# One attention and FFN kernel, one core: TensorE's order taken from a searched list

## The chip, the cores and the metric

The kernel runs on one core of a Trainium2 chip. The metric is the device time of one execution in microseconds, and the kernel before takes 229.23 us (median of 3 runs, 228.51 to 230.21). The *span* is the time from the first to the last instruction in the trace.

## The reference, cut to what matters

```python
B, H, S, D = 4, 8, 768, 64            # n_sink = 4, window = 128
keep = is_sink | in_window            # the first 4 keys, or the last 128
a = softmax(where(keep, q @ k.T / sqrt(D), -1e9));   x = a @ v
x = x.transpose(0, 2, 1, 3).reshape(3072, 512)
h = x @ w_in                          # 512 x 2048
g = h * sigmoid(beta * h)
out = g @ w_out                       # 2048 x 512
```

The kernel works on eight half batches of 384 tokens. A *unit* is one pair of heads of one half batch, so there are 32. The FFN of a half batch needs the attention of that half batch alone. That gives TensorE something to do while other engines work on the next attention.

## The kernel before

The program isn't written in its final order. Operations are added to a graph with their planned durations, and a planner inside the kernel's Python code decides which engine takes an operation that has alternatives and in which order each engine runs. The chip then executes these fixed orders, with semaphores. Before the change, TensorE's next group was decided by rules: at each step the first ready head of several streams, with margins, then a second pass that may pull one of eight groups ahead.

```python
while True:                                   # first pass: which stream next
    ...
    for s in tuple(PRIO) + ffn:               # OT, AV, SS, SC, T, then FFN
        h = head(s)
        if h[0] + mg <= now:
            best = (now, s, h[1]); break
    ...
for i, grp in enumerate(todo_pe[:self.SKIP]): # second pass: SKIP = 8
    ...
    if best is None or t < best[0] - self.SLACK:
        best = (t, "pe", i)
```

Some operations have alternatives with planned times (ns). They include a mask multiplication and a weight piece's cast from float32 to bf16:

```python
any_of(copies(dst, src_, {"act": 947, "dve": 602, "gp": 1060}), ...)    # one weight piece
any_of({"gp": (fn, 1150), "dve": (fn, 335)}, ...)                       # E * maskS
alts["dve"] = (lambda e: e.tensor_tensor(d, d, mk, ALU.mult), 70 + 256 * len(at_) / 1.9)   # E * maskT
add("sp", lambda e: e.dma_start(dst, src), 610, ...)                    # 192 KB of q or k
```

Weights arrive in 16 pieces of 512 KB. Half batches 0, 1 and 2 have q and k transposed by TensorE (`XB` = 3), and later ones by transposing DMAs ("crossbar"). Where the plan saw a gap at the start, TensorE got filler matmuls on a tile of ones.

The softmax here doesn't subtract the row's maximum and nothing guards it: scores larger than these inputs give would overflow.

Of the kernel before, what the change touches and what calls it, by code (L numbers as in the profile page):

```python
# [22 lines left out]
PAR = {'AHEAD': 0,  # L23
 'BACKLOG': 3000,
 'KEEP': 1000,
 'KEPT': 1,
 'MARGIN': 0,
 'MD': 1,
 'M_AV': 0,
 'M_H': 0,  # L30
 'M_O': 0,
 'M_OT': 500,
 'M_SC': 1000,
 'M_SS': 500,
 'M_T': 0,
 'PB': 2,
 'RAW': 0,
 'SPLIT': 0,
 'XB': 3,
 'l0': [4, 0, 3, 2, 1, 7, 5, 8, 10, 6, 9],  # L40
 'mix': 'awwwwwwwaawaaaaawaaawwawwwwwaaaa',
 'prio': ('OT', 'AV', 'SS', 'SC', 'T')}


class Op:
    __slots__ = ("eng", "fn", "deps", "signal", "count", "waits", "sem", "vc", "dma", "seq", "end", "ns", "alts",
                 "group", "tail", "preds", "ready", "left", "succ", "at", "queue", "ring", "lag")


class Graph:  # L50





    ENGINES = ("pe", "act", "dve", "gp", "sp")
    HOP = 180
    SKIP = 8
    SLACK = 50
    LEAD = 6000  # L60
    PAD = 1500
    BIAS, EARLY = 0, 10000

    COLD, WARM = 217, 150
    RING, FETCH = 165, 1100

    def __init__(self):
        self.ops = []
        self.writers = {}
        self.readers = {}  # L70
        self.last_x = {}
        self.reset()
        self.group = 0
        self.filler, self.fill_to = None, 0

    def reset(self):
        self.free = {e: 800.0 for e in self.ENGINES}
        self.dma_free = 0.0
        self.pending = []
        self.n_pe = 0  # L80

    def begin(self):

        self.group += 1

    def add(self, eng, fn, ns=0, r=(), w=(), x=(), dma=None, alts=None, queue=470, ring=64, lag=0, after=()):
# [3 lines left out]
        if alts:  # L90
            fn, ns = alts[eng]
        o.eng, o.fn, o.dma, o.ns, o.alts = eng, fn, dma, ns, alts or {eng: (fn, ns)}
        o.queue, o.ring, o.lag = queue, ring, lag
        o.signal, o.count, o.waits, o.vc = False, 0, [], None
        o.group = self.group if eng == "pe" else None
        o.seq = len(self.ops)
# [8 lines left out]
        for k in x:  # L105
            deps += [(p, False) for p in self.last_x.get(k, ())]
# [7 lines left out]
        for k in x:  # L114
            self.last_x[k] = [o] if eng == "pe" else self.last_x[k] + [o]
        at = self.free[eng]
        for p, _ in deps:
            at = max(at, p.end + (0 if p.eng == eng and not p.dma else self.HOP))
        self.place(o, at)
        self.ops.append(o)  # L120
        return o

    def fill(self, fn, r):

        def one():
            o = Op()
            o.eng, o.fn, o.dma, o.ns = "pe", fn, None, self.filler[0]
            o.signal, o.count, o.waits, o.vc = False, 0, [], None
            o.deps = [(p, True) for k in r for p in self.writers[k]]
            return o  # L130
        self.filler, self.fill_to = (self.COLD, one), self.group

    def place(self, o, at):
        o.at = at
        if o.dma:
# [11 lines left out]
            o.end = self.dma_free + 950 + (self.PAD if at > 45000 else 0)  # L147
        else:
            if o.eng == "pe":
                self.n_pe += 2  # L150
                if self.n_pe % 256 == 0:
                    self.dma_free = max(self.dma_free, at) + self.FETCH
            o.end = self.free[o.eng] = at + o.ns

    def at(self, keys):

        t = 0.0
        for k in keys:
            ws = self.writers.get(k)
            if not ws:  # L160
                return None
            t = max([t] + [p.end + self.HOP for p in ws])
        return t

    def bank_at(self, k):
        return max([0.0] + [p.end + self.HOP for p in self.last_x.get(k, ())])

    def arrange(self):


        ops = self.ops
        prev = None
# [6 lines left out]
        after = None  # L179
        for o in reversed(ops):  # L180
            o.tail = max([s.tail + self.HOP for s in o.succ] + [0.0])
            if o.eng == "pe":
                o.tail = max(o.tail, after.tail if after else 0.0)
                after = o
            o.tail += o.ns + (2000 if o.dma else 0)
        groups = {}
        for o in ops:
            if o.eng == "pe":
                groups.setdefault(o.group, []).append(o)
        todo_pe = list(groups.values())  # L190
        self.reset()
        new, planned = [], set()

        def ready(o, e):
            return max([0.0] + [p.end + (0 if p.eng == e and not p.dma else self.HOP) for p in o.preds])

        def done(o):
            planned.add(id(o))
            new.append(o)
            for s in o.succ:  # L200
                s.left -= 1
                if s.left == 0 and s.eng != "pe":
                    pool.append(s)

        pool = [o for o in ops if o.left == 0 and o.eng != "pe"]
        while todo_pe or pool:
            best = None
            for i, grp in enumerate(todo_pe[:self.SKIP]):
                own = set(map(id, grp))
                if any(id(p) not in planned and id(p) not in own for o in grp for p in o.preds):  # L210
                    continue
                t, off = self.free["pe"], 0.0
                for o in grp:
                    t = max([t] + [p.end + self.HOP - off for p in o.preds if id(p) not in own and p.eng != "pe"])
                    off += o.ns
                if best is None or t < best[0] - self.SLACK:
                    best = (t, "pe", i)
                if t <= self.free["pe"]:
                    break
            by_eng = {}  # L220
            for o in pool:
                opts = []
                for e, (fn, ns) in o.alts.items():
                    t = max(self.free[e], ready(o, e))
                    if o.dma:
                        t = max(t, self.dma_free - self.LEAD)
                    opts.append((t + ns + (self.BIAS if e == "act" and t < self.EARLY else 0), t, e))
                _, t, e = min(opts)
                by_eng.setdefault(e, []).append((t, o))
# [7 lines left out]
            if e == "pe":  # L237
                grp = todo_pe.pop(what)
                while self.filler and grp[0].group <= self.fill_to and self.free["pe"] + self.filler[0] <= t:
                    o = self.filler[1]()  # L240
                    self.place(o, max([self.free["pe"]] + [p.end + self.HOP for p, _ in o.deps]))
                    new.append(o)
                    if self.free["pe"] > 5000:
                        self.filler = (self.WARM, self.filler[1])
                if grp[0].group > self.fill_to:
                    self.filler = None
                for o in grp:
                    self.place(o, max([self.free["pe"]] + [p.end + self.HOP for p in o.preds if p.eng != "pe"]))
# [8 lines left out]
        for i, o in enumerate(new):  # L257
            o.seq = i

# [85 lines left out]
def bass_streamingllm_window__then__act_swish_beta_kernel(  # L345
# [34 lines left out]
    G.arrange()  # L380
# [13 lines left out]
def _program(nc, G, sb, ps, q, k, v, w_in, w_out, beta, out):  # L394
# [3 lines left out]
    RAW, PB = PAR.get('RAW', 1), PAR.get('PB', 2)  # L398
# [10 lines left out]
    def kind(hb):  # L409
        return "block" if hb in PARTS else "pair" if hb < PB else "whole" if hb < XB else "xbar"  # L410
# [4 lines left out]
    identF = sb("identF", (128, 128), F32)  # L415
# [27 lines left out]
    tt = sb("t", (128, HALF), F32, NTT)  # L443
    osb = sb("osb", (128, NOUT), F32, NOS)
    seen = sb("seen", (128, 12, 4), F32)
    G.touch = []
    G.touch.append((seen[:, 0:4, :], w_in.rearrange("(c p) f -> p c f", p=128)[:, :, 0:4]))
    G.touch.append((seen[:, 4:12, :], w_out.rearrange("(m p) n -> p m n", p=128)[:, 0:16:2, 0:4]))
# [8 lines left out]
    def tokens(hb, hp, i, rows, t0, n):  # L457
        if kind(hb) in ("pair", "whole"):
# [7 lines left out]
    def mark_t(hb, hps, cs):  # L466
        for hp in hps:
            for i in range(2):
                for c in cs:
                    G.writers["T", hb, hp, i, c] = G.writers["qkT", hb % (NT // 4), hp, i, c]  # L470

    def needs(u):
        hb, hp, c0, c1 = UNITS[u]
        ks = [c0 - 1] + list(range(c0, c1)) if c0 or hb % 2 else list(range(c0, c1))
        return [(hb if c >= 0 else hb - 1, hp, i, c % NK) for i, cs in ((0, range(c0, c1)), (1, ks)) for c in cs]

    def any_of(alts, r=(), w=(), x=()):

        return G.add(min(alts, key=lambda e: G.free[e] + alts[e][1] + (
            G.BIAS if e == "act" and G.free[e] < G.EARLY else 0)), None, 0, r, w, x, None, alts)  # L480
# [13 lines left out]
    w_in_src = w_in.rearrange("(c p) f -> p c f", p=128)  # L494
    w_out_src = w_out.rearrange("(m p) n -> p m n", p=128)
# [8 lines left out]
    held, kept = {7}, set()  # L504

    def choose(n):

        if n == 2:
            return min(((max(G.bank_at(("B", i)), G.bank_at(("B", i + 1))), [i, i + 1]) for i in range(7)
                        if not held & {i, i + 1}), default=None)  # L510
        if n == 4:
# [735 lines left out]
```

## Time and profile before

| | busy us | share of 226.9 us |
|---|---|---|
| TensorE | 216.4 | 95% |
| ScalarE | 153.8 | 68% |
| VectorE | 138.4 | 61% |
| GpSimd | 66.4 | 29% |

TensorE's 95% includes fillers and waits hidden inside pipelined matmuls. A better measure for this kernel, used in the prediction and below, is the *loss*. Take any matmul's start in the trace. Subtract what all useful matmuls ahead of it in the program occupy, by the start-to-start distances that the prediction lists (0.216 us for 512 columns, 0.187 us for entering and leaving a score block, and so on). What remains is time in which TensorE did nothing useful. In the kernel before, this loss is 7.7 us by 10 us, 12.5 by 20, 17.2 by 42, and 17.9 at the end.

### The profile page before, as it was taken

The numbers are of one execution on the slowest core, as the hardware profiler recorded it, in microseconds if no ns is written. First come the engines' busy times: TensorE is split into PE (matmuls) and PEld (weight loads), VectorE is DVE, ScalarE is ACT, GpSimd is POOL, SyncE is SP. The second block draws the span as 40 slices with busy tenths as digits, with TensorE's granted clock in tenths as the row PEclk, the third lists the DMA queues.
The fourth block names the chain that finished last, engine by engine and source line by source line (L and its number), as shares of the span: only waits on it lengthen the run. The fifth ranks groups of instructions, "written<-read, shape, count | busy, mean of one in ns | idle before, by whom it ended". The sixth has DMA issues, their size and how long they took to land.

```text
span 226.9 us, 4543 instructions
## 1 busy us (share of the span) xinstructions
PE 216.4 (95%) x1746; PEld 123.1 (54%) x1769; DVE 138.4 (61%) x304; ACT 153.8 (68%) x277; POOL 66.4 (29%) x155
## 2 busy tenths in 40 slices
PE   7979878999999999999999999999999999999994
PEld 5655446456555565655555555545554565555543
DVE  2898969756894678826887666654452455733310
ACT  2878998449786777748887756676585776744441
POOL 8450455012222663432225541020243630000000
PEclk9999999999999999999999999999999999999999
DMA  7999999999969999999999999511113121011112
GB/s 163 265 364 361 339 248 337 350 282 238 226 121 240 215 227 233 230 219 220 196 252 196 229 208 207 136 49 46 35 49 81 49 81 35 4 46 46 46 49 92
DMA packets 95845, 39.78 MB, mean 175 GB/s; under 512 B 82368, under 2 KB 88784, under 8 KB 95824
## 3 DMA queue, kind: packets, MB, share of 16 engines
q1 hardware_dynamic: 94256, 39.47, 74.1%
q8 instruction: 14, 0.23, 0.4%
q10 hardware_dynamic: 1568, 0.02, 0.4%
q14 instruction: 7, 0.06, 0.1%
HBM read 27.30 MB, written 6.29 MB: 148 GB/s over the span
## 4 chain that ended last, share of the span: by engine, by line
PE 81%; DVE 9%; ACT 5%; DMA 2%; issue 1%; SPq 0%
PE P L942 36%; PE P L920 32%; PE P L791 4%; PE P L871 4%; DVE onorm L878 2%; DVE g L927 2%; ACT E L800 2%; ACT t L925 2%; DMA k_stage<-in_k_dram 2%; PE P L861 1%; PE P L828 1%; PE P L700 1%; DVE k L543 1%; DVE E L817 1%; ACT qkT L538 1%
## 5 line engine op out<-in xcount | busy, mean ns | idle before, releaser
L925 ACT ACTIVATE t<-P,hbeta 128x384 f32<-128x384 f32 x128 | 73.2, 585 | 38.7 <-PE P L920 33.4
L927 DVE SCALAR_TENSOR_TENSOR g<-t,P 128x384 bf16<-128x384 f32 x128 | 69.1, 550 | 45.7 <-ACT t L925 43.9
L920 PE MATMUL P<-xT,w_in 128*128 128x384 bf16 x512 | 96.1, 326 | 0.0
L942 PE MATMUL P<-w_out,g 128*128 128x512 bf16 (+2 forms) x377 | 90.4, 370 | 1.2
L806 POOL TENSOR_SCALAR_AFFINE_SELECT E<-E 128x256 bf16<-128x256 bf16 x109 | 54.5, 529 | 94.1 <-ACT E L800 93.7
L920 PEld LDWEIGHTS P<-xT,w_in 128*128 128x128 bf16 x512 | 48.5, 98 | 36.8 <-DVE w_in L543 0.6
L942 PEld LDWEIGHTS P<-w_out,g 128*128 128x128 bf16 x400 | 36.8, 98 | 35.0 <-issue 0.5
L800 ACT ACTIVATE E<-P 128x768 bf16<-128x768 f32 x64 | 45.7, 768 | 4.1 <-PE P L791 4.1
L538 ACT ACTIVATE osb<-P 128x512 f32<-128x512 f32 (+2 forms) x24 | 13.9, 581 | 14.1 <-PE P L942 13.9
L871 PE MATMUL P<-vaug,E 128*128 128x65 bf16 x352 | 18.6, 193 | 1.4 <-DVE vaug L543 1.4
L871 PEld LDWEIGHTS P<-vaug,E 128*128 128x128 bf16 x352 | 16.6, 97 | 4.3 <-DVE vaug L543 1.7
L878 DVE TENSOR_TENSOR onorm<-P,rden 128x384 bf16<-128x384 f32 x32 | 17.8, 556 | 0.9
L791 PE MATMUL P<-qkT 64*128 64x128 bf16 (+1 forms) x256 | 15.9, 239 | 0.4 <-ACT E L800 0.2
L832 ACT ACTIVATE ES<-P 128x128 bf16<-128x128 f32 (+1 forms) x32 | 12.0, 402 | 4.3 <-PE P L828 4.3
L791 PEld LDWEIGHTS P<-qkT 64*128 64x128 bf16 x256 | 8.5, 94 | 11.2 <-issue 5.6
L876 DVE RECIPROCAL rden<-P 128x6 f32<-128x6 f32 x32 | 6.1, 191 | 12.5 <-PE P L871 12.4
L543 DVE CAST vaug<-v_stage 128x512 bf16<-128x512 f32 x22 | 10.8, 491 | 3.6 <-DMA v_stage<-in_v_dram 3.4
L543 DVE CAST q<-q_stage 128x512 bf16<-128x512 f32 (+1 forms) x20 | 9.6, 484 | 5.2 <-DMA q_stage<-in_q_dram 5.2
L861 PE MATMUL P<-vS,ES 128*128 128x130 bf16 x64 | 12.7, 221 | 0.0
L817 DVE TENSOR_TENSOR E<-E,maskS 128x512 bf16<-128x512 bf16 x16 | 7.7, 482 | 5.9 <-ACT E L800 5.1
L543 DVE CAST k<-k_stage 128x512 bf16<-128x512 f32 (+1 forms) x20 | 9.3, 469 | 3.0 <-DMA k_stage<-in_k_dram 2.9
L1173 PE MATMUL P<-ones 128*128 128x256 bf16 x44 | 8.8, 341 | 1.1 <-POOL ones L549 1.1
(50 smaller groups left out, 93.2 us busy)
## 6 DMA issues: line engine op xcount, KB each, us to landing
v_stage<-in_v_dram SPq DMA_DIRECT2D x24, 256.0 KB, 4.8
out_dram<-osb SPq DMA_DIRECT2D x23, 256.0 KB, 2.6
q_stage<-in_q_dram SPq DMA_DIRECT2D x15, 256.0 KB, 4.7
k_stage<-in_k_dram SPq DMA_DIRECT2D x15, 256.0 KB, 5.1
wst<-in_moe_w_in_dram SPq DMA_DIRECT2D x5, 512.0 KB, 6.9
wst<-in_moe_w_out_dram SPq DMA_DIRECT2D x4, 512.0 KB, 8.7
g<-in_moe_w_out_dram SPq DMA_DIRECT2D x4, 512.0 KB, 7.0
q_stage<-in_q_dram SPq DMA_DIRECT2D x8, 192.0 KB, 6.0
```

What stands on the lines that cost most here:

```text
L538: return lambda e: e.activation(dst, src, AF.Copy, bias=0.0, scale=scale)
L543: return lambda e: e.tensor_copy(dst, src)
L791: add("pe", lambda e, dst=dst, own=own, kc=kc, rows=rows, q0=q0, nq=nq: e.matmul(dst, tokens(own, hp, 1, rows, kc, 1)[:, 0, :], tokens(hb, ...
L800: add("act", lambda e, src=src, dst_=dst_: e.activation(dst_, src, AF.Exp, bias=0.0, scale=SCALE), act_ns(256 * n), w=[(k_, z, j) for k_ i ...
L806: alts = {"gp": (lambda e, d=d, sg=sg, at_=at_: e.affine_select(d, d, [[0, 2 * len(at_)], [sg, 128]], ALU.is_ge, 0.0, base=min(sg, 0), cha ...
L861: add("pe", lambda e, m=m, o0=o0: e.matmul(A[:, o0:o0 + 2 * (D + 1)], ES[z][:, (c0 + m) * 128:(c0 + m + 1) * 128], vS[b % 2][:, 2 * hp:2 * ...
L871: e.matmul(A[:, o0:o0 + D + 1], E[z][:, i, hh, :], vaug[vz][:, kb % NK, 2 * hp + hh, :], start=a, stop=o, skip_group_check=True), 39,
L878: add("dve", lambda e: e.tensor_tensor(onorm[:, on, 2 * c0:2 * c1, :], av[:, :, 0:D], rden[on][:, 0:2 * nb].unsqueeze(2).to_broadcast([128 ...
L920: add("pe", lambda e, c=c: e.matmul(hp, w_in16[:, c, m * 128:(m + 1) * 128], xT[:, hb, c, 128 * c0:128 * c1], start=(c == 0), stop=(c == 3 ...
L925: add("act", lambda e: e.activation(tt[ti][:, 0:n], hp, AF.Tanh, bias=0.0, scale=hbeta[:, m:m + 1]), act_ns(n) + 93, r=["hbeta"], w=[("t", ...
L927: add("dve", lambda e: e.scalar_tensor_tensor(gt[hb % NG][:, m, 128 * c0:128 * c1], tt[ti][:, 0:n], 1.0, hp, ALU.add, ALU.mult), dve_ns(n) ...
L942: add("pe", lambda e, m=m: e.matmul(P[:, bk, a:b], gt[hb % NG][:, m, t * 128:(t + 1) * 128], w_out16[:, m, a:b], start=(m == 0), stop=(m = ...
```

## The change

TensorE's order is now one string, with one letter for a group: T q/k transposes, C and D the two halves of a unit's scores, S sink scores, A attention times V, X output transposes, h and g the halves of an early FFN group, H a whole one, O a quarter of the second FFN. The list was found by a search outside the kernel. Half batch 2 goes by crossbar (`XB` = 2). Fillers go into any planned gap of TensorE up to 48 us. The rest of the planner stays greedy: other engines still take what is ready first. Three smaller things came along: another order of the first loads (`l0`, `mix`), a handicap of 300 ns on ScalarE where an operation has alternatives (`BIAS`), and new planned latencies.

```diff
-    best over todo_pe[:self.SKIP]            # rules choose TensorE's next group
+    g = todo[at_pe]                          # the list does
 ...
+ORDER = ('TCDTSTTDCSDSCASCTADACbXXAhhhXXThghDghgDhggThgggChhgghgShDSghSghghTghgCASCAXADOXO...')
-    'XB': 3,
+    'XB': 2,
 ...
     for c in range(4):                       # first FFN, one tile
+        if c == 2 and hb < 2:
+            G.begin("g")                     # second half is a group of its own
 ...
+    def fillers(self, t, banks, holder, new):
+        while self.free["pe"] < min(t, self.FILL_TO):
+            n = min(512, int((t - now) * 2.4 / slow) // 128 * 128)
+            if not free or n < 128:
+                return                       # no filler in a gap under 128 columns
-    HOP = 180
+    LAT = {"act": 108, "dve": 85, "gp": 45, "pe": 163, "sp": 0}      # ns, by engine
+    HOP = {"act": 37, "dve": 33, "gp": 67, "pe": 57, "sp": 26}
```

PSUM banks are now chosen in the same pass.

## The prediction

> **What bounds the kernel now.** I first read the busy time of each engine in a few stretches of the span (start:end in us, then busy us and count for each engine, granted TensorE clock, DMA share, GB/s).
>
> ```profile
> 10.00:20.00 10.00, 8.46 (x107) 5.19 (x105) 9.05 (x24) 7.94 (x16) 4.31 (x10) 1.00 1.09 345
> 20.00:30.00 10.00, 8.23 (x69) 4.68 (x67) 9.94 (x22) 9.50 (x18) 2.32 (x4) 1.00 1.14 325
> 30.00:40.00 10.00, 8.36 (x113) 5.64 (x115) 7.36 (x19) 9.21 (x17) 6.17 (x12) 1.00 0.96 307
> 40.00:220.00 180.00, 178.73 (x1360) 99.09 (x1382) 107.36 (x234) 120.86 (x219) 47.53 (x101) 1.00 0.71 152
> 220.00:227.00 7.00, 3.99 (x35) 2.54 (x32) 0.00 (x0) 1.37 (x3) 0.00 (x0) 1.00 0.23 80
> ```
>
> From 40 to 220 us TensorE is busy 178.73 of 180 us: there only fewer or cheaper matmuls help. Before 40 us it is not the only limit: VectorE is at 9.05 and 9.94 of 10, ScalarE at 9.50 and 9.21, DMA is full.
>
> Busy TensorE is not useful TensorE, so second I read, in the timeline of TensorE, the distance from one start to the next (start us, us, what). The first lines are the filler matmuls on a tile of ones, the others show what a useful matmul occupies.
>
> ```profile
> 1.06 3.81 PE L1173 MATMUL P<-ones 128*128 128x256 bf16 x17 [1.06 <-POOL ones L549]
> 4.66 0.53 PE L700 MATMUL P<-ident,q 128*128 128x128 bf16 x3
> 5.54 0.50 PE L700 MATMUL P<-ident,k 128*128 128x128 bf16 x3 [0.36 <-DVE k L543]
> 5.84 1.19 PE L1173 MATMUL P<-ones 128*128 128x256 bf16 x6
> 6.95 0.45 PE L791 MATMUL P<-qkT 64*128 64x256 bf16 x8
> ...
> 17.77 4.33 PE L920 MATMUL P<-xT,w_in 128*128 128x384 bf16 x24
> ...
> 40.15 2.54 PE L942 MATMUL P<-w_out,g 128*128 128x512 bf16 x11
> ```
> ```profile
> 66.25 0.81 PE L920 MATMUL P<-xT,w_in 128*128 128x384 bf16 x4
> ...
> 70.63 1.03 PE L942 MATMUL P<-w_out,g 128*128 128x512 bf16 x4
> 71.50 0.65 PE L828 MATMUL P<-qkT,kS 128*128 128x384 bf16 x3
> ...
> 72.37 0.81 PE L942 MATMUL P<-w_out,g 128*128 128x512 bf16 x3
> 73.11 0.45 PE L791 MATMUL P<-qkT 64*128 64x256 bf16 x8
> 73.49 0.82 PE L942 MATMUL P<-w_out,g 128*128 128x512 bf16 x3
> ```
>
> 70.63 to 71.50 is 0.87 for four: 0.216 us a 512-column matmul. The same reading gives 0.163 at 384 columns, 0.057 at 130, 0.056 at 128, 0.029 at 65; score matmuls (64 rows, two side by side) 0.058 and 0.028 each. Three L942 take 0.648, but 72.37 to 73.11 is 0.74: entering a block of 64-row matmuls costs 0.09 more. The block (0.28 of its own) lasts to 73.49, so leaving costs as much: 0.187 for each block.
>
> Useful work, by the counts of the built program: 512 x 0.163 (first FFN) + 368 x 0.216 + 16 x 0.163 + 16 x 0.056 (second FFN) + 352 x 0.029 + 64 x 0.057 (attention times V) + 96 x 0.058 + 160 x 0.028 (scores) + 16 x 0.163 + 16 x 0.056 (sink scores) + 109 x 0.056 (transposes) = 200.0 us; with 32 score blocks x 0.187 = 6.0 it is **205.9 us**. (The program has 1,769 matmuls, the profile 1,746: 23 records are missing, so I count in the program.)
>
> The span is 226.9. The last matmul ends at 224.0; eviction and output take the last **3.0**. That leaves 18.0 us of TensorE without useful work. Up to the first L942 at 40.15 the program holds 22.7 us of useful work, so **17.4 us are lost before 40 us and 0.6 after**. Of the 17.4: 1.06 before the first filler, 7.0 in fillers (17 in 1.06 to 4.66, six in 5.84 to 6.95, 21 more at 0.107), and 9.3 in waits. The stretch from 17.77 to 40.15 holds 17.1 us of work in 22.4, so 5.2 of those waits lie after the fillers end.
>
> **What the Trainium skill says.** "TensorE: Matmul & The Clock Gate", Back-to-back issue gap, gives N/2.4 + 2.5 ns warm and N/1.2 cold. The trace agrees: 216 and 163 ns for 512 and 384 columns, and the first 17 fillers take 212 ns each against 107 for 256 columns later. "TensorEngine Tiling (Array Packing)", Key Properties: changing the tiling mode drains TensorE. The 0.09 us on either side of a score block is that. "Advanced Engine Details and Errata", X-Bar Transpose (TRN2), says transposing DMAs are about as fast as plain ones. The trace's DMA list agrees roughly: 4.1 and 4.4 us median from issue to landing for a q or k transpose of 384 KB, 4.7 to 5.1 for a 256 KB load.
>
> **The change part by part.**
> (1) Half batch 2 by crossbar. Its 24 q/k transposes and 12 of the normalized output leave TensorE: 36 x 0.056 = **-2.0 us**, all on the path. Evictions saved: four of 0.8 to 0.9 us and four of 0.35 to 0.49, beside other work. Added: four transposing DMAs near 50 to 65 us.
> (2) Halves of scores. The built program has 37 score blocks instead of 32: 5 x 0.187 = **+0.9 us**. Useful work becomes 205.9 - 2.0 + 0.9 = **204.9**.
> (3) Order and early FFN halves. FFN matmuls of half batch 0 now start after two of its four output transposes, and mix with half batch 1's scores, instead of 24 in a row behind all four transposes. This goes at the 9.3 us of waits. Nothing can come from after 40 us: only 0.6 is lost there.
> (4) Fillers: 31 instead of 44, but up to 512 columns wide: 15,104 columns = 6.3 us warm. About nine wide ones run cold (the clock is slow to about 4.8 us) and take 0.43 instead of 0.21: 8.2 us in all. They now stand wherever the plan expects a gap up to 48 us, so they replace waits rather than add to them. If the plan held exactly, the loss would be 1.1 + 8.2 = **9.3 us** instead of 17.4.
>
> **How much of that is real.** I check against VectorE. Up to the eighth normalization (end of half batch 1's attention) it does in the new order, by distances between starts in its old timeline: 16 gate products x 0.475 = 7.6; 8 normalizations with reciprocals x 0.69 = 5.5; 13 q/k casts x 0.40 = 5.2; 8 weight casts x 0.60 = 4.8; 4 transposed evictions x 0.87 = 3.5; 5 V casts, 4 sink masks, 3 masks, 5 xT copies and small ones about 6.3. Sum 32.9, near the old amount. By 10 us it had done 4.65; 28.3 remain, and at the 95% that it reached from 10 to 30 us they take 29.8: 39.8 us. The transpose that needs this stands in the new order after 27.7 us of useful work (in the old one after 25.3). So at least about 12 us are lost by then. I choose **12.7**: this bound plus a little for unplanned waits, above the plan's 9.3.
>
> Sum: 204.9 + 12.7 + 1.0 (later waits, a little more than now for the new transposes) + 3.0 = 221.6 us of span. Measured times lie above the span by 2.3 (229.23 against 226.9) or 1.8 (228.72 for the profiled run); with 1.9 I get **223.5 us**, a gain of 2.5%.
>
> **The rivals.**
> *VectorE and ScalarE stay the bound, and order buys little.* For: 9.94 and 9.50 of 10 us from 20 to 30. Against: VectorE idles 2.6 us from 30 to 40, and weight casts move to GpSimd, which is busy 2.32 of 10 there. With 15 to 16 us still lost: 226 to 227.
> *DMA arrival.* The last w_out piece follows two half batches (4.7 MB), 8.4 MB of weights and three loads of half batch 2 (0.8): 13.9 MB. The trace moved 2.1 MB by 10 us and then 0.32 MB a us: 46.8. It is wanted after 36.4 us of useful work, near 49. It fits with two microseconds spare; if not, 1 to 2 us more.
> *The crossbar for half batch 2 is late.* Its k pieces come after the last w_out piece (49 us), then a cast and two transposes of 4.1 and 4.4: 56 to 58. The first sink scores want them after 44.1 us of useful work, at 56.8. A stall up to 2 us is possible and would eat the 2.0 saved: 225.5.
> *The plan holds exactly.* 9.3 + 1 lost: 220.
>
> **Range and chances.** Two percent is 224.6, only 1.1 above my number, so the sign is safer than the class. The four outcomes span 220 to 227. Range 220.5 to 226.8; faster 0.70, within 2% 0.28, slower 0.02, as TensorE's work is smaller and the fillers replace waits.
>
> **What would show it.** Right: first L931 (second FFN) near 35 to 36 us; TensorE again above 99% busy from 45 to 215; useful work plus about 12.7 lost before 45 us; the tail still 3 us. Wrong: waits of TensorE for ScalarE or VectorE of more than 6 us in total between 15 and 45; a wait for a q or k transpose near 57; more score switching than 37 blocks; or a gain found after 60 us, which this reasoning excludes.

## The result

The changed kernel takes 226.66 to 227.11 us (median 226.7, 4 runs), and the kernel before took 228.94 (228.51 to 230.21) beside it. The ratio is 0.9897 with a 95% interval of 0.9855 to 0.9939. Here and below a ratio is the mean time of one kernel's fast runs over that of the other's in the same rounds, so not quite the ratio of the medians. So the change gains 1.1%, where 2.5% was predicted. The time lies inside the range, 0.1 us under its upper end, and of the classes the one that was given 0.28, within 2%, is what came.

The stretches that the prediction showed of before, for the changed kernel (columns as there):

```profile
10.00:20.00 10.00, 8.88 (x108) 5.72 (x107) 9.37 (x26) 8.57 (x17) 7.31 (x16) 0.83 1.09 322
20.00:30.00 10.00, 10.00 (x82) 5.57 (x79) 8.60 (x17) 8.75 (x16) 3.29 (x7) 1.00 1.07 334
30.00:40.00 10.00, 9.28 (x103) 5.54 (x101) 10.00 (x24) 8.49 (x16) 5.25 (x9) 1.00 0.97 278
40.00:220.00 180.00, 177.69 (x1347) 97.80 (x1365) 108.91 (x241) 111.92 (x203) 45.62 (x102) 1.00 0.77 161
```

From 20 to 30 us TensorE is now busy throughout (8.23 before). VectorE, the third column, is at 10.00 of 10 from 30 to 40, where it had 2.6 us to spare. GpSimd went from 4.31 to 7.31 between 10 and 20. After 40 us TensorE is busy 177.69 instead of 178.73. The 0.83 is a spell of lower clock, which later runs of the same kernel don't have at the same time.

TensorE's timeline, with the lines that answer to those of before:

```profile
6.96 0.34 PE L697 MATMUL P<-ident,k 128*128 128x128 bf16 x3 [1.24 <-DVE k L563]
...
19.90 1.14 PE L910 MATMUL P<-xT,w_in 128*128 128x384 bf16 x6
...
38.43 0.81 PE L931 MATMUL P<-w_out,g 128*128 128x512 bf16 x3
```

The first k transpose comes at 6.96 instead of 5.54 and the first FFN matmul at 19.90 instead of 17.77, so the new kernel is *behind* until 20 us. Then it mixes FFN matmuls with the next half batch's work and overtakes: the second FFN starts at 38.43 instead of 40.15. The prediction said 35 to 36.

The loss at six points, in us:

| by | before | after |
|---|---|---|
| 10 us | 7.7 | 8.6 |
| 20 us | 12.5 | 13.6 |
| 42 us | 17.2 | 15.2 |
| 60 us | 17.2 | 15.2 |
| 90 us | 17.4 | 17.15 |
| end | 17.9 | 17.45 |

So against the kernel before, the new schedule loses 1.1 us up to 20 us and wins 3.1 from 20 to 42. Between 60 and 90 its loss grows by 1.95, where before it grew by 0.2. The net is 0.4. With 1.1 less useful work (205.94 to 204.86) that makes the 1.5 us by which the span shrank, from 226.9 to 225.4. (The changed kernel's profiled run is the slowest of its four, and before's is one of its quicker ones. By the ratio the gain is 2.4 us.)

The stretch from 74 to 83 us of the changed kernel, all engines (start, duration, engine, what, and in brackets the idle time and what ended it):

```profile
75.63 3.32 SPq L635 DMA_DIRECT2D v_stage<-in_v_dram  x3
...
78.12 0.69 DVE L564 TENSOR_SCALAR osb<-P 128x512 f32<-128x512 f32 x1 [2.81 <-DMA out_dram<-osb]
...
80.48 0.43 DVE L563 CAST vaug<-v_stage 128x512 bf16<-128x512 f32 x1 [1.66 <-DMA v_stage<-in_v_dram]
...
81.46 1.05 ACT L915 ACTIVATE t<-P,hbeta 128x384 f32<-128x384 f32 x2 [2.08 <-DVE g L917]
...
82.69 0.85 PE L931 MATMUL P<-w_out,g 128*128 128x512 bf16 x2 [0.36 <-DVE g L917]
```

VectorE runs in its fixed order. An output eviction waits 2.81 us for an output buffer to be stored, then a V cast waits 1.66 us for its load, one of three issued from 75.63 on. The FFN's gate products stand behind both, ScalarE waits for them, and TensorE waits last.

### The profile page after: what moved, and what is told of

Its sections match the earlier page's. It is cut to its first block, busy times and chain, and to the rows that moved or that the text cites.

```text
span 225.4 us, 4463 instructions
## 1 busy us (share of the span) xinstructions
PE 216.1 (96%) x1699; PEld 119.9 (53%) x1720; DVE 141.0 (63%) x313; ACT 141.6 (63%) x257; POOL 66.4 (29%) x157
## 4 chain that ended last, share of the span: by engine, by line
PE 70%; DVE 10%; SPq 8%; DMA 6%; ACT 3%; issue 1%
PE P L931 31%; PE P L910 28%; SPq L635 7%; DMA v_stage<-in_v_dram 5%; DVE g L917 4%; PE P L861 4%; PE P L783 3%; DMA out_dram<-osb 2%; PE P L851 2%; SPq L891 1%; ACT t L915 1%; PE P L819 1%; PE P L1027 1%; DVE onorm L868 1%; DVE vaug L563 1%
## 5 line engine op out<-in xcount | busy, mean ns | idle before, releaser
L910 PE MATMUL P<-xT,w_in 128*128 128x384 bf16 x512 | 92.7, 327 | 0.0
L915 ACT ACTIVATE t<-P,hbeta 128x384 f32<-128x384 f32 x128 | 71.8, 586 | 32.3 <-PE P L910 24.4
L931 PE MATMUL P<-w_out,g 128*128 128x512 bf16 (+2 forms) x379 | 89.1, 371 | 1.7 <-DVE g L917 0.4
L798 POOL TENSOR_SCALAR_AFFINE_SELECT E<-E 128x256 bf16<-128x256 bf16 (+1 forms) x109 | 52.4, 512 | 57.7 <-ACT E L792 57.7
L931 PEld LDWEIGHTS P<-w_out,g 128*128 128x128 bf16 x400 | 36.6, 98 | 37.5 <-DVE g L917 1.5
L792 ACT ACTIVATE E<-P 128x768 bf16<-128x768 f32 (+1 forms) x64 | 45.6, 760 | 14.8 <-PE P L783 14.7
L558 ACT ACTIVATE osb<-P 128x512 f32<-128x512 f32 (+2 forms) x16 | 9.1, 570 | 15.2 <-PE P L931 15.1
L868 DVE TENSOR_TENSOR onorm<-P,rden 128x384 bf16<-128x384 f32 x32 | 17.4, 552 | 0.5
L563 DVE CAST k<-k_stage 128x512 bf16<-128x512 f32 (+1 forms) x24 | 11.5, 477 | 6.0 <-DMA k_stage<-in_k_dram 5.7
L563 DVE CAST vaug<-v_stage 128x512 bf16<-128x512 f32 x18 | 7.9, 439 | 8.2 <-DMA v_stage<-in_v_dram 8.0
L725 POOL TENSOR_TENSOR kS<-qkT,headm 128x8 bf16<-128x8 bf16 x16 | 3.0, 209 | 32.5 <-DMA qkT<-k 28.8
L1027 PE MATMUL P<-ones 128*128 128x512 bf16 (+2 forms) x31 | 9.8, 443 | 1.2 <-POOL ones L569 1.1
L564 DVE TENSOR_SCALAR osb<-P 128x512 f32<-128x512 f32 x9 | 6.2, 690 | 6.9 <-DMA out_dram<-osb 5.2
```

The costliest lines, as they stand in the source:

```text
L563: return lambda e: e.tensor_copy(dst, at())
L792: add("act", lambda e, src=src, dst_=dst_: e.activation(dst_, src(), AF.Exp, bias=0.0, scale=SCALE), act_ns(256 * n), w=[(k_, z, j) for k_ ...
L798: alts = {"gp": (lambda e, d=d, sg=sg, at_=at_: e.affine_select(d, d, [[0, 2 * len(at_)], [sg, 128]], ALU.is_ge, 0.0, base=min(sg, 0), cha ...
L868: add("dve", lambda e: e.tensor_tensor(onorm[:, on, 2 * c0:2 * c1, :], av()[:, :, 0:D], rden[on][:, 0:2 * nb].unsqueeze(2).to_broadcast([1 ...
L910: first = add("pe", lambda e, c=c: e.matmul(hp(), w_in16[:, c, m * 128:(m + 1) * 128], xT[:, hb, c, 128 * c0:128 * c1], start=(c == 0), st ...
L915: add("act", lambda e: e.activation(tt[ti][:, 0:n], hp(), AF.Tanh, bias=0.0, scale=hbeta[:, m:m + 1]), act_ns(n) + 93, r=["hbeta"], w=[("t ...
```

## How the plan and the chip differ

The planner leaves a planned start for every instruction, and each engine runs in the planned order. So the planned start can be set beside the start in the trace, instruction by instruction. I call the difference the *slip*. On VectorE of the changed kernel it is 1.1 us at the first k cast, 1.25 at 13 us, 2.7 to 3.0 from 19 to 20 us, then about level up to 60 us. It goes up to 5.6 at 80 us and is back at 2.7 at the end. And the plan itself isn't free of loss: by the same reckoning, planned times hold 12.2 us of loss by 39 us (42 us on the chip) and 14.8 at the end. 12.2 + 3.0 is the 15.2 measured at 42 us. So two questions are left for experiments. Where do the 3.0 us come from, and does getting them back shorten the run?

The slip has two parts. The first 1.1 us is the first loads. The planner counts 0.61 us for each 192 KB piece. In the trace the first three q casts, each waiting for its load, start at 3.70, 4.78 and 5.82 us. For the 1.9 us between 13 and 19 us I suspected this (VectorE and GpSimd, timeline of the changed kernel):

```profile
15.77 1.05 POOL L560 TENSOR_SCALAR_AFFINE_SELECT w_in<-wst 128x1024 bf16<-128x1024 f32 x1 [0.71 <-DMA wst<-in_moe_w_in_dram]
15.93 1.16 DVE L809 TENSOR_TENSOR E<-E,maskS 128x512 bf16<-128x512 bf16 x1
17.12 0.24 DVE L803 TENSOR_TENSOR E<-E,maskT 128x256 bf16<-128x256 bf16 x1
17.59 1.04 POOL L560 TENSOR_SCALAR_AFFINE_SELECT w_in<-wst 128x1024 bf16<-128x1024 f32 x1
18.05 0.72 DVE L803 TENSOR_TENSOR E<-E,maskT 128x256 bf16<-128x256 bf16 x1
```

The same multiplication (L803) takes 0.24 us at 17.12 and 0.72 at 18.05, where GpSimd's weight cast has just begun. At 15.93 the maskS multiplication takes 1.16; without a cast beside it, it takes 0.39 at 14.95. Both end 0.1 to 0.3 us after GpSimd's cast does. The Trainium skill's page "SBUF — State Buffer", Who interferes with whom, describes it: "A DVE instruction with two SBUF inputs contends with a GpSimd instruction that reads SBUF", but not with one that only writes it. It calls the ports that the two engines share an exclusive lock. The planner counts each engine alone.

A smaller part of the 1.9 us arises between 13 and 14 us:

```profile
12.83 2.23 POOL L798 TENSOR_SCALAR_AFFINE_SELECT E<-E 128x256 bf16<-128x256 bf16 x5 [0.50 <-ACT E L792]
13.18 0.79 DVE L686 COPY vS<-vaug 4x260 bf16<-4x260 bf16 x2
```

Two copies of 0.20 us each in the plan take 0.79 together while GpSimd masks.

## The experiments

Sixteen runs, each timed in five rounds beside the kernel before. The changed kernel itself was run again (after_again and after_b below). osb_act, osb9, l0_pairs, before_xb2, cast_nolock, ffn_rs, scores_rs and xb3_rs are compared with it through their ratios to before. They were run at other times. The list can stay the same while the plan does not: in each of these programs the planner runs anew, and the other engines can get another order.

### The later stall: osb_act, osb9

```diff
-        any_of(copies(osb[z]..., {"dve": ..., "act": ...}, 0.5), ...)
+        any_of(copies(osb[z]..., {"act": ...}, 0.5), ...)          # osb_act
+    osb += [half of each weight staging tile]; NOS = 9            # osb9, nine buffers instead of three
```

> Output evictions on ScalarE alone instead of 9 of 24 on VectorE. Theory (in-order VectorE: an eviction that waits for an output buffer, whose output DMA sits behind loads, holds up the V cast and the gate products behind it): VectorE no longer idles 2.40 and 2.81 us on out_dram from 74 to 81 us, the loss between 74 and 87 us falls from 1.9 to under 0.6, and the time falls by about 1.4 us to some 225.3. Rival (the late v_stage load is what holds VectorE, 1.66 us before the V cast at 80.48): the V cast still waits, the loss stays above 1.3, time 226.2 to 227.

> Nine output buffers instead of three (six of them the weight staging, free by then), VectorE may still evict. Theory of the output buffer: the same gain as osb_act, about 1.4 us, as no eviction waits for an output DMA. Rival of the late v_stage load: under 0.5 us gained.

osb_act: 229.05 us, ratio 0.9981 (0.9951 to 1.001). osb9: 228.43 us, ratio 0.9959 (0.9923 to 0.9994). In osb_act the stall is gone: the loss grows 0.45 us from 75 to 90 us instead of 1.45. Yet the run is about 2 us *longer* than the changed kernel. ScalarE took the nine evictions of VectorE, and now 0.6 to 1.0 us is lost in each of three later places, near 117, 127 and 161 us. osb9 loses 1.25 us from 70 to 90 us, no less than the changed kernel (1.2 to 1.6 in its three profiles), and 1.2 between 115 and 130. From 60 to 95 us VectorE no longer waits for an output store in either run, but waits 6.4 and 6.8 us for V loads (1.7 in the changed kernel). So the stall was real, but removing one of its causes moved the wait. In osb9, as the rival said, the V load holds VectorE. The plans, run again from the recorded kernels, say the rest: TensorE ends at 221.95 us in osb_act's plan and at 220.8 in osb9's, against 219.66, so 2.3 and 1.1 us of the lengthening (about 1.9 and 1.4 measured) was planned.

### The late first k transpose: l0_pairs

```diff
-PAR = {..., 'l0': [0, 2, 6, 1, 3, 4, 9, 5, 7, 10, 8], ...}
+PAR = {..., 'l0': [0, 1, 2, 3, 4, 5, 6, 7, 8, 9, 10], ...}       # first loads in q, k pairs
```

> Half batch 0 loaded as q0 k0 q1 k1 ... v v v instead of the searched q0 q1 q3 k0 k1 q2 v ...; nothing else in the text. Theory (the later first k, cast-ready at 6.96 instead of 5.54 us, is a loss that nothing pays back): the first k transpose moves to about 5.5 us, the loss at 20 us falls from 13.6 to about 12.5, time falls by about 1 us to 225.7. Rival (the start is set by the last loads, V and k3, and by VectorE after them, which the order of the first does not change): the loss at 20 us stays within 0.4 of 13.6, time within 0.5 of 226.7 or worse.

230.77 us, ratio 1.0056 (1.0025 to 1.0087). The first k transpose does start at 5.38 us, as the theory said. The loss is 0.6 us smaller by 10 us, equal at 24 us, and 1.5 larger by 42, and the kernel is 3.6 us slower than the changed one. Starting k earlier doesn't help here. But the planner decided otherwise after it, and its plan for this program (run again) ends 2.8 us later, so this isn't the load order alone.

### The crossbar alone, and the crossbar undone: before_xb2, xb3_rs

```diff
-    'XB': 3,
+    'XB': 2,           # before_xb2: in the kernel BEFORE
-PAR = {..., 'XB': 2, ...}
+PAR = {..., 'XB': 3, ...}   # xb3_rs: in the changed kernel, four T and four X more in the list, list searched anew
```

> The kernel before with half batch 2 by crossbar, one parameter. If the removed 36 transposes (2.0 us of TensorE work) count in full: 227.0. If the crossbar's transposes of half batch 2 bring a wait of their own in the full DMA queue near 55 to 90 us, as I suspect for part of the loss after the change: 228 to 230.

> Half batch 2 transposed by TensorE again, as before, under a list searched anew. Useful work 206.7 instead of 204.9, plan ends at 222.9 instead of 219.7. Theory (the saved transposes lie wholly on TensorE's path): 1.8 to 3.5 us slower than the changed kernel, 228.5 to 230.5. Rival (crossbar transposes cost as much in waits as they save): within 1 us of it.

before_xb2: 233.68 us, ratio 1.0178 (1.0148 to 1.0209). Useful work fell by 2.4 us and the loss rose by 7.4; between 60 and 90 us alone the kernel loses 6.4 us, where before loses 0.2. xb3_rs: 231.57 us, ratio 1.0091 (1.0065 to 1.0117), 4.5 us over the changed kernel. Useful work rose by 1.8 us, as expected, and the rest is loss (19.9 instead of 17.0 to 17.6). The 4.5 us are more than the expected 1.8 to 3.5. Under the old rules the crossbar for half batch 2 costs more than it saves, and the old planner, run again, plans this itself: its planned loss at the end rises from 18.9 to 25.2 us. With the lists it doesn't. The 1.8 us of transposes come back when it is undone; how much of the other loss is the crossbar's and how much the new search's, this run doesn't show.

### The changed kernel again: after_again, after_b

> The changed kernel again, unaltered, on the chip of the other runs of this job, to compare them with. The planner inside the kernel sets every instruction's order from planned times; in the trace the first start of each instruction can be set beside its planned start ('slip'). In the profiled run before, the slip of VectorE was 1.1 us at the first k cast, 2.8 to 3.0 at 20 us and 2.7 at the end. Expected here: 226.3 to 227.3 us, slip at 20 us 2.8 to 3.1.

> The changed kernel once more, for comparison within this job: 226.5 to 227.5 us, slip of VectorE against the plan 2.8 to 3.1 us at 20 us.

after_again: 227.21 us (226.71 to 228.29), ratio 0.9897 (0.9869 to 0.9925). after_b: 226.9 us (226.13 to 228.3), ratio 0.9891 (0.9856 to 0.9926). Both profiled runs had full clock between 14 and 18 us, and their slip from 19 to 20 us was 2.7 to 3.1 all the same, so the spell of low clock in the first profile explains none of it. In both, a maskT multiplication takes 1.12 us beside GpSimd's first weight cast.

### Keeping weight casts off GpSimd: nogp_early

```diff
-any_of(copies(dst, src_, {"act": 947, "dve": 602, "gp": 1060}), ...)
+any_of(copies(dst, src_, {"act": 947, "dve": 602} if j < 4 else {..., "gp": 1060}), ...)
```

> The first four casts of w_in may no longer go to GpSimd (in the changed kernel two of them run there for 1.05 us each, from 15.8 and 17.6 us, and a mask multiplication on VectorE that starts in each takes 1.16 and 0.72 us instead of 0.42 and 0.26). The plan itself becomes 2.55 us longer by this, as VectorE and ScalarE take the casts. Theory (VectorE's multiplications wait while GpSimd runs, and that is the plan's slip between 13 and 19 us): slip at 20 us falls from 3.0 to about 1.8, and the time is only about 1.4 us over the changed kernel's. Rival (the slip comes from late loads or from TensorE's cold clock): slip at 20 us stays 2.8 to 3.1 and the time is 2.5 us over.

232.57 us (230.66 to 233.78), ratio 1.0118 (1.0076 to 1.0161): a miss, 5.1 us over the changed kernel. From 15 us on the multiplications did take 0.28 to 0.41 us, and VectorE's slip stayed at 1.8 until 17.8 us. But in the profiled run TensorE's granted clock was 0.50 between 16 and 18 us, VectorE waited 1.11 us for TensorE's transposes before 18.91, and the slip was 2.8 to 3.0 from 19 to 20 us. Two runs at a clock of 0.999 to 1.0 took 230.7 and 231.0, the other four (0.985 to 0.993) 232.5 to 233.8. The casts also went to VectorE and ScalarE. This run couldn't separate the causes.

### Fillers: no_fill

```diff
-    FILL_TO = 48000
+    FILL_TO = 0
```

> No fillers at all: TensorE idles in the gaps. By the plan this is 1.65 us longer (other bank choices). Theory that fillers keep the clock: the granted clock from 10 to 35 us falls well under 0.8 and the loss by 42 us grows by 2 us or more beyond the plan, total 230 or more. Rival (start is bound by VectorE and ScalarE, TensorE's clock does not matter there): the loss by 42 us is the plan's, time 227.5 to 229.

231.92 us, ratio 1.009 (1.0063 to 1.0118). The loss by 20 us is 13.7, by 42 us 15.7, against 13.6 and 15.3 with fillers. Meanwhile TensorE ran at half speed until about 17 us (its timeline; three 128-column transposes take 0.50 us where the warm kernel shows 0.33):

```profile
4.49 0.50 PE L697 MATMUL P<-ident,q 128*128 128x128 bf16 x3 [4.49 <-POOL vaug L579]
...
15.05 0.50 PE L697 MATMUL P<-ident,q 128*128 128x128 bf16 x3
```

So in this kernel half speed up to about 17 us adds 0.1 us of loss by 20 us, and fillers gain nothing there. (In nogp_early, half clock from 16 to 18 us did hold VectorE.) The rest was lost in four steps of 1.1 to 1.9 us between 85 and 155 us, where neither kernel has fillers. Without them the planner decides otherwise from the start on (its plan is 1.65 us longer). Neither expectation was met: the cold start cost hardly anything, and the time was still 4.4 us over the changed kernel's. Why the later steps are so large is open.

### The exclusion counted in the plan: lock

```diff
+                    if e == "gp" or e == "dve" and o.tag == "sh":
+                        t = max(t, self.pair)      # busy until the other's instruction ends
```

> Same list, but the planner counts GpSimd's instructions and VectorE's casts, vS copies and mask multiplications as excluding each other. The plan is then 5.1 us longer (TensorE ends at 224.8 instead of 219.7). Theory (the lock is most of the slip between 13 and 19 us): slip at 20 us 0.5 to 1.5 and at the end about the same, so 228 to 229.5 us, or under it where the plan is too careful. Rival (loads or clock): slip at 20 us stays 2.8 to 3.1, time 230.5 or more.

231.61 us, ratio 1.0095 (1.006 to 1.0131). The slip is 1.05 at 13 us and 0.5 to 1.3 from there to 50 us: with the exclusion counted, the chip follows the plan after the first loads. The two vS copies take 0.45 us here, not 0.79. The theory of the slip holds; the forecast of the time (228 to 229.5) doesn't. The kernel is 4.5 us slower than the changed one, about as much as its plan is longer (5.1).

### GpSimd's casts that read nothing: cast_nolock, cast_nolock_b

```diff
+        alts = copies(dst, src_, {"act": 947, "dve": 602, "gp": 1060})
+        alts["gp"] = (lambda e: e.memset(dst, 0.01), 1060)     # wrong result on purpose
```

> Wrong results on purpose: where GpSimd casts a piece of w_in it now only writes a constant (a memset of the same tile), so that it reads nothing from SBUF; plan, list and the order on every engine stay those of the changed kernel. Theory (VectorE's mask multiplications were held while GpSimd's two w_in casts read SBUF): VectorE's slip at 20 us falls from 2.9 to about 1.8, TensorE's loss at 42 us from 15.3 to about 14.1, the time by about 1 us, to 225.5 to 226.2. Rival (loads or the clock make the slip): slip 2.8 to 3.1, time unchanged. If the clock falls to half between 14 and 18 us in the profiled run, part of the slip may come back from that.

> The kernel with GpSimd's w_in casts as memsets again (wrong results on purpose): its profiled run had a slip of 1.65 at 20 us and took 225.43 us, its other five took 227.3 to 227.9. Theory (the held multiplications are worth 1.2 us, and where a run does not get them something else, such as the half clock between 14 and 18 us, takes their place): the profiled run shows a slip near 1.7 if its clock is full in 14 to 18 us, and near 2.7 with TensorE's own work late if it is half; runs spread again from 225.4 to 228. Rival (the first profiled run was a stray): slip near 2.9 whatever the clock, and mask multiplications of over 0.7 us again.

The plan and every engine's order are those of the changed kernel; only what GpSimd does in a weight cast differs. cast_nolock: 227.68 us (225.43 to 227.9), ratio 0.9904 (0.9869 to 0.994). cast_nolock_b: 226.54 us (225.95 to 227.36), ratio 0.9873 (0.9845 to 0.9901). The timeline of cast_nolock_b, VectorE and GpSimd:

```profile
14.95 0.95 POOL L658 MEMSET w_in<- 128x1024 bf16 x1
15.14 0.28 DVE L805 TENSOR_TENSOR E<-E,maskT 128x256 bf16<-128x256 bf16 x1
...
15.81 0.41 DVE L811 TENSOR_TENSOR E<-E,maskS 128x512 bf16<-128x512 bf16 x1
...
16.24 0.24 DVE L805 TENSOR_TENSOR E<-E,maskT 128x256 bf16<-128x256 bf16 x1
```

GpSimd is busy for 0.95 us (1.05 in the cast), but it reads nothing from SBUF, and the multiplications beside it take 0.28 and 0.41 us. Both runs agree on the start and differ after it:

| loss by | after_b | cast_nolock | cast_nolock_b |
|---|---|---|---|
| 20 us | 13.5 | 12.3 | 12.2 |
| 60 us | 15.1 | 14.2 | 14.4 |
| 90 us | 16.7 | 15.5 | 16.1 |
| end | 17.0 | 15.75 | 16.95 |

The start gains 1.2 to 1.3 us in both. In cast_nolock's profiled run, the fastest of its six, the gain reaches the end. In cast_nolock_b's it is gone: 0.6 us is lost at 41 us, 1.1 between 70 and 80 us and 0.7 between 140 and 170. The other five runs of cast_nolock took 1.8 us or more over its fastest, without a trace to show where. Why some executions keep the gain and others don't is not settled. Over all fast runs no gain in time is shown: cast_nolock's ratio is 0.9904 and cast_nolock_b's 0.9873, where the changed kernel has 0.9897, 0.9897 and 0.9891, and the intervals overlap. The theory's time, 225.5 to 226.2, was missed by both medians. In cast_nolock_b, the stall after 74 us again shows VectorE in fixed order waiting for an output store (2.96 us) and a V load (0.83 us), with the DMA engines at or over full share (1.12 from 70 to 80 us, 1.34 from 80 to 90).

### The halves: scores_rs, ffn_rs, ffn_rs2

```diff
-ORDER = (... C and D of a unit in different places; h and g ...)
+ORDER = (... CD always together ...)                 # scores_rs, list searched anew
+ORDER = (... H in place of h and g ...), 'HS': 0      # ffn_rs2, list searched anew
```

> Both halves of a unit's scores always next to each other again (32 score blocks instead of 37), list searched anew. Plan: TensorE ends at 220.1 instead of 219.7, useful work 204.0 instead of 204.9. Theory (score halves buy about what their switching costs): 0 to 1.5 us slower than the changed kernel, 227 to 228.5. Rival (they are what cut the waits): 229 or more.

> FFN matmuls of the first two half batches in whole groups of four again instead of halves; list searched anew for this by the kernel's own planner (45 minutes of small moves), since the old list is worth nothing for other groups. Plan: TensorE ends at 220.4 instead of 219.7, useful work 204.3 instead of 204.9 (three score blocks fewer), planned loss 13.2 at 39 us. Theory (halves of the FFN are worth under 1 us): 0 to 1.5 us slower than the changed kernel, 227 to 228.7. Rival (the halves are what cut the start's waits): 229 or more.

> The run ffn_rs was given the wrong file: whole FFN groups under the old list with the halves struck out, whose plan ends at 222.3, not the list searched anew. This is the one that was meant: plan 220.4 (+0.7), useful work 204.3. Theory (halves of the early FFN are worth under 1.5 us): 227 to 228.7 us. Rival (they are what cuts the start's waits, whatever the list): 229 or more.

scores_rs: 229.09 us, ratio 0.999 (0.9968 to 1.0012). ffn_rs is another file than its text says, with the old list and the halves struck out, whose plan is 2.6 us longer. It took 233.95 us, ratio 1.0203. ffn_rs2 is the kernel that was meant: 230.72 us, ratio 1.0044 (1.0021 to 1.0067). By the times, score halves are worth about 2 us and FFN halves about 3.5, and by the times that they named (229 or more) the rivals won in both, for scores_rs by 0.1 us. By the loss it is less clear. At 56 us scores_rs had lost 16.05 us and ffn_rs2 16.2, against 15.2, so about 1 us more at the start, and both have less useful work (0.9 and 0.6 us over the whole run). Most of ffn_rs2's deficit arises after 60 us, where the loss rises by 5.8 us. So "undo one part" also tests my own shorter search. The times are therefore likely upper limits for the parts, and how much the original search had gained beyond its own plan stays open.

### An attempt at a better kernel: dmacast_rs

```diff
+        add("gp", lambda e: e.dma_start(w_in16_piece, src), ...)   # float32 in HBM, bf16 in SBUF
-        cast_w(j)                                                  # no engine casts weights
```

> An attempt at a better kernel: all 16 weight pieces are cast to bf16 by the transfer itself, issued from GpSimd's queue, so that no engine casts weights; list searched anew (25 minutes). The plan ends at 219.7 like the changed kernel's. Theory (the start is bound by VectorE's work and by GpSimd's casts holding it): slip at 20 us 1.5 to 2, so 225.3 to 226.2 us. Rival (transfers that GpSimd issues cost GpSimd more, or land later, than planned): slip over 3, 228 or more.

The transfers are issued from GpSimd's queue, and the result is correct. It took 229.62 us (22 runs, 228.01 to 231.41 and one slow run of 233.22), ratio 1.0012 (0.9988 to 1.0036). The profiled run is the fastest of them. Up to 20 us it does what the theory says: slip 1.5, loss 12.2. Then TensorE waits for weights (the waits of TensorE between 22 and 46 us: total, times, longest):

```profile
PE P L913 <- DMA w_in<-in_moe_w_in_dram: 1.4, 2, 1.2
PE P L934 <- DMA w_out<-in_moe_w_out_dram: 0.7, 1, 0.7
```

VectorE is down to 6.99 of 10 us between 20 and 30 and 2.92 between 40 and 50. The share of the DMA engines between 20 and 30 us is 1.24, where the changed kernel has 1.07. (Their GB/s can't be compared. The profile counts a casting transfer by what it writes, 256 KB a piece instead of 512. With the other half added, 14.1 MB moved from 5 to 50 us, against 13.8.) The last weight piece lands at 50.9 us; in the changed kernel it lands at 49.5 and is cast by 50.3. The loss by 42 us is 15.8. With VectorE relieved, TensorE waits for weights that still land as late, as the rival said in part; its slip of over 3 came only after 30 us.

## Why the prediction was right or wrong

**Useful work: right.** 204.9 us was predicted from counts. The loss is defined by subtracting it, so the end of the span is no check of it. A better one is that from 90 us to the last matmul, 132 us later, the loss grows by only 0.3 us, so the costs per matmul can't be far off. The section Back-to-back issue gap, which the prediction quotes, gives its formula for a matmul alone, and for a stream of weight loads and matmuls it has about 131 ns at 512 columns. This case's stream takes 216, so the formula is what fits here. That the 2.0 us of transposes lie on TensorE's path is made likely by xb3_rs, where 1.8 us come back, but its list is another one.

**"If the plan held exactly, the loss would be 1.1 + 8.2 = 9.3 us": wrong.** I took fillers for the plan's whole loss. The planner puts no filler into a gap under 128 columns, and its planned times hold 12.2 us of loss by 39 us, fillers included, and 2.6 more after it. This step made the rival "the plan holds exactly: 220" too low, and it made 12.7 look like a cautious number when it was nearly the plan itself.

**"I choose 12.7": the term that failed most, 15.2 measured.** The direction was right: the loss before 45 us fell. But it was to fall from 17.4 to 12.7, and it fell from 17.2 to 15.2. What failed is "this bound plus a little for unplanned waits": the bound of 12 was a lower bound, and the waits above it came to 3 us. That 12.7 lay close to the plan's own 12.2 was luck. I worked with mean durations, and let VectorE run at 95% from 10 us on. In the trace it starts 1.1 us late because of the first loads (3.70, 4.78 and 5.82 us), and it loses 1.9 us more between 13 and 19 us. The largest part of the latter is one that the change itself made: it put two weight casts on GpSimd there (the kernel before has none on GpSimd up to 46 us), which hold VectorE's two-input multiplications for 0.3 to 0.9 us each. I listed "weight casts move to GpSimd" as a relief. It is one for VectorE's work but not for its waits. cast_nolock and cast_nolock_b show this part as 1.2 to 1.3 us of loss at 20 us, of which 0.7 to 1.0 is left by 42 to 60 us. The two vS copies add 0.4, and in lock, with the exclusion counted, no other slip appears there. The 1.1 us of the first loads is read from the trace; no run removes it.

**The first rival came true in size.** "15 to 16 us still lost: 226 to 227" is what was measured. VectorE went to 10.00 of 10 us from 30 to 40, and no_fill shows that TensorE's half speed up to 17 us costs hardly anything. "Order buys little" is right of the end alone: the new schedule saved 3.1 us from 20 to 42, and 0.4 of loss is left of it at the end.

**"1.0 (later waits)" : 2.25 measured.** The plan held 2.6 for them. The largest is the stall from 74 to 87 us, fed by DMA: an output store and a V load that VectorE, in fixed order, waits for. osb_act removes most of the stall and ends later nonetheless, as its plan does. I had looked for a late crossbar near 57 us and for w_out; neither stalled TensorE for long.

**Tail and offset: right.** 2.9 us after the last matmul (3.0 predicted), and 1.7 us from span to time (1.9). The 2.3 that the prediction also gives sets the median against the span of another run; 1.8 is that of its own run.

The sum: 2.5 us more at the start, 1.2 more later and 0.1 less in the tail make the span 225.4 instead of 221.6 (from rounded terms), less 0.2 in the offset.

Of the signs that I named for being right, two failed: the first L931 came at 38.43 us instead of 35 to 36, and TensorE was 98.7% busy from 45 to 215 us (167.80 of 170), not above 99%. Of those for being wrong, none came. The one that was meant for this failure, waits for ScalarE or VectorE of more than 6 us in total between 15 and 45, shows only this in the list of TensorE's waits (total, times, longest):

```profile
PE P L851 <- DVE qkT L563: 0.3, 1, 0.3
PE P L819 <- ACT ES L823: 0.2, 1, 0.2
PE P L861 <- DVE vaug L563: 0.2, 1, 0.2
```

Seven fillers (2.36 us) stand where waits would be, and matmuls whose end is modelled cover more: TensorE counts as busy for 29.10 of these 30 us. By the loss, about 4.4 us went there, also under 6. So the sign was set where this failure couldn't reach it. A gain found after 60 us didn't occur; a loss did, and the reasoning had left no room for one.

## What to carry to other kernels

When a kernel is ordered by a plan, set the planned starts beside the traced ones, and find the first place where they part: here 3 us by 20 us, carried with small changes to the end. Don't read a plan's loss from its fillers alone: take it from the plan itself, which can be run before the chip. Where one detail is changed, first see how much longer the plan becomes (2.3, 1.1 and 2.8 us for osb_act, osb9 and l0_pairs). A searched order fits one program exactly: eleven runs that changed one detail of this program, with the old list or with one that I searched for minutes, and kept the right result, all came out slower than it, by about 1.5 to 7 us.

## What the Trainium skill lacked or had wrong

- "SBUF — State Buffer", Who interferes with whom, was right, and I hadn't used it: multiplications of two SBUF tiles took 0.56 to 1.16 us beside a GpSimd cast instead of 0.24 to 0.41, and were not held by a 0.95 us memset. No page says how the cost of such a hold is carried: 1.2 to 1.3 us at 20 us, of which 0.05 to 1.25 us was left at the end of the two profiled runs.
- "TensorE: Matmul & The Clock Gate", What's actually happening, has the clock slow until sustained work. The runs agree (half speed to about 17 us without fillers), but the profile's granted clock reads 1.00 over that whole stretch in no_fill, and 0.52 in 16 to 18 us of the changed kernel. The page's section Seeing it yourself does warn that the throttle's events in a trace are unreliable. It doesn't say that a cold start can be missed whole; durations have to be read instead.
- "DMA: Bandwidth & Descriptors", SWDGE vs HWDGE vs iDMA, says where a casting DMA must be issued but gives no rate for one. With all 16 weight pieces cast this way, they landed in 7.2 us (w_in) and 5.9 us (w_out) in the median, against 6.7 to 9.5 for plain ones, and the last landed at 50.9 us instead of 49.5. The profile counts such a transfer at its bf16 size.
